# Softmax divided on the product with the values instead of on its own tiles

## The chip, the cores and the metric

The kernel runs on one core of a Trainium2 chip. The metric is the device time of one execution in microseconds (us). TensorE (PE in the rows; PEld is its weight load) multiplies, VectorE (DVE), ScalarE (ACT) and GpSimd (POOL) work element by element, and SyncE (SP) issues the transfers.

## The reference

Attention in which a query sees only the keys of its own hash bucket, and then a feed-forward layer with a convolution along the sequence. B, H, S, D = 4, 8, 768, 64; model width 512, hidden width 1024.

```python
mask = q_bucket[:, :, :, None] == k_bucket[:, :, None, :]
scores = np.where(mask, scale * (q @ k.T), -1e9)
attn = np.exp(scores - scores.max(-1))
attn = attn / (attn.sum(-1) + 1e-9)
x = attn @ v                              # (B, S, H * D)
h = np.maximum(x @ w_in, 0)
gate = sigmoid(conv3(h, conv_w))          # along the sequence, per channel
out = (h * gate) @ w_out
```

## The kernel before

The work is written in one order by hand, and every engine takes its own instructions in that order. A **pair** is two heads of a batch (16 pairs). A **unit** is 128 queries of one head against all 768 keys (192 units, 12 to a pair). The main loop takes one unit a turn and works on three units at once:

- `products` (L250) makes the scores of unit i on TensorE, four matmuls into one of three PSUM buffers "S". The mask is in the product, by extra rows of the operands.
- `maximum` (L258) takes the row maximum on VectorE and writes the scores to SBUF as tile `e`; L262 scales the maximum. `total` (L265) adds 1e-9 to the sum of the unit before.
- `exponential` (L268) is ScalarE's: exp of `e`, with the row sum as a second result.
- `normalise` of unit i-1: the reciprocal of its sum on VectorE (L273), then on GpSimd `e` times it, 128 x 768 (L274).
- `transposes` of unit i-3 (L279) are six transposes of 128 x 128 on TensorE into the next "S" buffer, and `to_sbuf` (L286) is ScalarE's copy of them. Since products and transposes take the three buffers in turn, the transposes of a turn take the buffer which the maximum of the turn before has read.
- Four units (two heads, 256 queries) make one **product with the values**: 24 matmuls of 256 columns (`values`, L299), run in one turn of four (`AVS`). In the next turn ScalarE rounds the result to `xh` (L304), and in the turn after VectorE makes the rest `xl` (L307), at the end of its turn. There are 48 products.

Called by their place against the products, the turns repeat in fours: the first turn after a product with the values, the second (with L307 in it), the third, and the fourth, at whose end the next product runs. In what follows one such four is a **period**.

Beside this run a pair's preparation (`split`, `hash`: GpSimd's L168, L173 and L188, VectorE's L186, transfers) and, until the first feed-forward, the decoding of the 16 weight blocks from float64: VectorE's L88, L90, L92, L94 and L96 on tiles of 128 x 512, ScalarE's L86 and L104, GpSimd's L106 and L108. They are dealt out a step a turn, a block every 4.1 turns, each behind the turn's attention work on the same queues.

The feed-forward of a batch is put off by two pairs (`DEFER`). It runs as one block of work, four times, and takes along (`fill`) the last product with the values of the pair that has just ended. Its hidden part is L324 to L343, its output L354 to L362. The last one follows the last pair, and uses what that pair has just made.

Of the kernel before, what the change touches and what calls it, by code (L numbers as in the profile page):

```python
# [7 lines left out]
F32 = mybir.dt.float32  # L8
# [4 lines left out]
ALU = mybir.AluOpType  # L13

B, H, S, D = 4, 8, 768, 64
NB = 6
DM, DFF = 512, 1024
P = 128
NP = H // 2
NCK = S // P  # L20
HS = S // 2
QB = 256
# [7 lines left out]
LAG, EB = 3, 5  # L30
DEFER = 2
FLAG = 3
AVS = (6, 0, 0, 0)
PREP = (3, 2, 1)
PREP_N = 6
W0 = 6
# [6 lines left out]
def lsh_attention_conv_ffn(ctx, tc, qk, v, hw, w_in, conv_w, w_out, consts, ident_in, out):  # L43
    nc = tc.nc
    PSUM = bass.MemoryType.PSUM
    cp = ctx.enter_context(tc.tile_pool(name="const", bufs=1))
    wp = ctx.enter_context(tc.tile_pool(name="work", bufs=1))
# [4 lines left out]
    def ring(pool, bufs, shape, dtype, tag, name):  # L52

        k = turns[tag] = (turns.get(tag, -1) + 1) % bufs
        return pool.tile(shape, dtype, tag=f"{tag}{k}", name=name, bufs=1)


    ident = cp.tile([P, P], F32, name="ident")
# [51 lines left out]
    def decode_taps(raw):  # L110
        up, low = yield from decode(raw, NFC * 3, "cw")
        nc.vector.tensor_tensor(cw.rearrange("p f k -> p (f k)"), up, low, ALU.add)
# [7 lines left out]
    def fetch(n):  # L120

        for src, name in blocks[:n]:
            raw = cp.tile([P, 2 * WC], I32, tag=f"w{name}", name=f"raw{name}")
            nc.sync.dma_start(raw, src)
            fetched.append((raw, name))
        del blocks[:n]

    def background(rate, stop):

        step[0] += 1  # L130
        if rate and fetched and step[0] // rate > (step[0] - 1) // rate:
            splits.append(split_weight(*fetched.pop(0)))
        now = splits[:]
        while now:
            for g in now[:]:
                ended = next(g, None)
                if ended is None:
                    splits.remove(g)
                if ended is None or ended >= stop:
                    now.remove(g)  # L140
# [97 lines left out]
    class Unit:  # L238
# [11 lines left out]
                    nc.tensor.matmul(self.sp[:, half, :HS], A[:, h, qs], C[:, h, half * HS:(half + 1) * HS],  # L250
                                     start=(kk == 0), stop=(kk == 1))

        def maximum(self, prev):

            self.st = ring(wp, 8, [P, 4], F32, "st", f"st{self.nm}")
            e = wp.tile([P, 776], F32, tag="e", name=f"e{self.nm}", bufs=EB)
            self.e = e[:, :S]
            nc.vector.tensor_scalar(self.e.rearrange("p (a b) -> p a b", a=2), self.sp[:, :, :HS],  # L258
                                    MASKED, None, ALU.max, ALU.max, accum_out=self.st[:, 0:1])
            if prev:  # L260
                prev.total()
            nc.vector.tensor_scalar(self.st[:, 1:2], self.st[:, 0:1], -SCALE, None, ALU.mult)  # L262

        def total(self):
            nc.vector.tensor_scalar(self.st[:, 2:3], self.st[:, 2:3], 1e-9, None, ALU.add)  # L265

        def exponential(self):
            nc.scalar.activation(self.e, self.e, AF.Exp, bias=self.st[:, 1:2], scale=SCALE,  # L268
                                 accum_out=self.st[:, 2:3])

        def normalise(self):
            st = self.st
            nc.vector.reciprocal(st[:, 3:4], st[:, 2:3])  # L273
            nc.gpsimd.tensor_scalar(self.e, self.e, st[:, 3:4], 0.0, ALU.mult, ALU.add)  # L274

        def transposes(self):
            self.tp = ring(ps, 3, [P, 2, 512], F32, "S", f"t{self.nm}")
# [8 lines left out]
            nc.scalar.copy(pr.at[self.h][:, :, :, self.tq * P:(self.tq + 1) * P],  # L286
                           self.tp[:, :, :3 * P].rearrange("p j (c q) -> p j c q", c=3))

    def values(pr, qb, ats):

        if qb == 0:
            pr.x = [ring(wp, NP + DEFER, [P, S], F32R, f"x{k}", f"x{k}{pr.nm}")
                    for k in "hl"]
        vt, (xh, xl) = pr.v, pr.x
        av = ring(ps, 2, [P, 512], F32, "M", f"v{pr.nm}_{qb}")

        def chunk(c):
            for h in range(2):
                nc.tensor.matmul(av[h * D:(h + 1) * D, :QB], vt[:, c, h, :],  # L299
                                 ats[h][:, c // 3, c % 3, :],  # L300
                                 start=(c == 0), stop=(c == NCK - 1), tile_position=(0, h * D))

        def out_high():
            nc.scalar.copy(xh[:, cols], av[:, :QB])  # L304

        def out_low():
            nc.vector.tensor_tensor(xl[:, cols], av[:, :QB], xh[:, cols].bitcast(F32), ALU.subtract)  # L307

        cols = slice(qb * QB, (qb + 1) * QB)
        return [lambda c=c: chunk(c) for c in range(NCK)], (out_high, out_low)  # L310


    g2, prep = [None], [iter(())]
# [54 lines left out]
    def ffn(b, xs, fill, last):  # L368

        gs, acc, run = [], {}, []  # L370
        load_table(AF.Sigmoid)
        todo = [(half, f) for half in range(2) for f in range(NFC)]
        for i in range(len(todo) + FLAG):
            if i < len(todo):
                run.append(hidden(b, *todo[i], xs))
                next(run[i])
            if 1 <= i <= len(todo):
                next(run[i - 1], None)
            if i == 0:
                fill()  # L380
            fetch(1)
            background(HRATE, 2)
            if i >= 3:
                next(prep[0], None)
            if i == len(todo):
                load_table(AF.Exp)
            if i == len(todo) + FLAG - 1:
                last()
            if i >= FLAG:
                output(b, *todo[i - FLAG], gs[i - FLAG], acc)  # L390
            if i < len(todo):
                gs.append(next(run[i]))
            background(HRATE, 2)
# [3 lines left out]
    units = [Unit(pr, t, h) for pr in pairs for qb in range(S // QB) for h in range(2)  # L397
             for t in range(qb * QB // P, (qb + 1) * QB // P)]
# [8 lines left out]
    av, outs, lows, early = [], [], [], None  # L407
    n = len(units)
    ffn_after = {min((b + 1) * NP - 1 + DEFER, B * NP - 1): b for b in range(B)}
    for i in range(n + LAG):  # L410
        u = units[i] if i < n else None
        before = units[i - 1] if 1 <= i <= n else None
        w = units[i - LAG] if i >= LAG else None
        pi, k = divmod(i, 2 * NCK)
        done, outs, lows = lows, [], outs
        for high, low in lows:
            high()
        wi = (i - LAG) // (2 * NCK)
        ending = w and wi in ffn_after and w.qb == S // QB - 1
        if u:  # L420
            u.products()
        if ending:
            for high, low in done + lows:
                low()
            done, lows = [], []
        if u:
            u.maximum(before)
        elif before:
            before.total()
        if w and w is not early:  # L430
            w.transposes()
            w.to_sbuf()
        if u:
            u.exponential()
        if i in (0, 2):
            next(first, None)
        if before:
            before.normalise()
        for high, low in done:
            low()  # L440
        for _ in range(NCK if ending else AVS[(i - LAG) % 4]):
            if av:
                steps, last = av[0]
                steps.pop(0)()
                if not steps:
                    outs.append(last)
                    av.pop(0)
        if u and k == PREP[min(pi, 2)] and pi + 1 < len(pairs):
            prep[0] = pairs[pi + 1].prepare()
        next(prep[0], None)  # L450
        if u and k == PREP[min(pi, 2)] + PREP_N and pi + 1 < len(pairs):
            pairs[pi + 1].load_v()
            if pi + 2 < len(pairs):
                pairs[pi + 2].load()
        if i == 3:
            splits.append(decode_taps(cwr))
        if i >= W0 - 4:
            fetch(i % 4 == 2)
        if i >= 1:
            background(RATE if i >= W0 else 0, 1)  # L460
        if w and w.tq == QB // P - 1 and w.h == 1:
            if not ending:
                av.append(values(w.pair, w.qb, w.pair.at))
            else:
                def fill():
                    steps, last = values(w.pair, w.qb, w.pair.at)
                    for step in [*steps, *last]:
                        step()

                bi = ffn_after[wi]  # L470
                early = units[i + 1 - LAG] if i + 1 - LAG < n else None

                def transposes_ahead():
                    if early:
                        early.transposes()
                        early.to_sbuf()
                        turns["S"] -= 1

                ffn(bi, [pairs[bi * NP + c].x for c in range(NCC)], fill, transposes_ahead)
# [43 lines left out]
```

## Time and profile before

| | |
|---|---|
| median of 3 runs | 774.25 us (772.6 to 776.9) |
| time of the profiled execution | 775.63 us |
| its span, first to last instruction | 773.8 us |
| PE, DVE, ACT, POOL busy | 93%, 65%, 66%, 52% |
| mean granted TensorE clock | 0.98 |

Busy time is a mean over stages with different limits: until 230 us the weights are decoded beside the attention, then four feed-forwards alternate with stretches of attention alone. A wait is read in the stretch where it falls.

### The profile page before, as it was taken

Reading aid. Unit: us, or ns where it says so; the run is one execution under the profiler, and the core shown is the slowest. Engines: PE = TensorE matmul, PEld = TensorE weight load, DVE = VectorE, ACT = ScalarE, POOL = GpSimd, SP = SyncE. Lnnn points to the kernel's source line nnn. Section 1 sums busy time; section 2 is a strip of 40 time slices with the busy share of each in tenths; the row PEclk is TensorE's granted clock in tenths of the full one; section 3 lists DMA queues with packets and bytes.
Section 4 is the critical chain, followed back from the end, with each engine's and each line's share of the span. In section 5 each row is a group of like instructions: output and inputs, shape, how many; then the busy total and the mean of one; then the engine's idle time right before and its main releaser. Section 6 shows DMA issues by size and latency. Waiting matters only on the chain.

```text
span 773.8 us, 13581 instructions
## 1 busy us (share of the span) xinstructions
PE 721.3 (93%) x4552; PEld 586.1 (76%) x4552; DVE 506.7 (65%) x1320; ACT 510.7 (66%) x954; POOL 399.5 (52%) x373
## 2 busy tenths in 40 slices
PE   6968888787889999999999999999999999999997
PEld 3746667565668988777778998777778998778986
DVE  8858988777686665566665655656665665654653
ACT  5857767675665556777775556877776556875453
POOL 4749869595864423557553523466553523441322
PEclk9989999998999999999999999999999999999999
DMA  4565565473631212155452312064452311000011
GB/s 136 141 179 144 153 178 144 135 177 97 153 86 47 62 41 103 38 155 121 119 146 50 82 41 102 19 174 105 132 149 49 82 42 61 1 2 1 1 42 41
DMA packets 30357, 72.18 MB, mean 93 GB/s; under 512 B 5936, under 2 KB 7504, under 8 KB 30288
## 3 DMA queue, kind: packets, MB, share of 16 engines
q1 hardware_dynamic: 30000, 71.27, 33.9%
q8 instruction: 36, 0.59, 0.3%
q14 instruction: 33, 0.27, 0.1%
q10 hardware_dynamic: 288, 0.05, 0.0%
HBM read 27.40 MB, written 6.29 MB: 44 GB/s over the span
## 4 chain that ended last, share of the span: by engine, by line
PE 81%; DVE 10%; issue 3%; DMA 3%; POOL 1%; ACT 1%; SPq 0%; DVEq 0%; POOLq 0%
PE h L324 17%; PE o L354 17%; PE v L299 17%; PE s L250 14%; PE t L279 14%; DVE e L258 5%; DMA R<-in_qk 2%; PE hash L183 2%; DMA k<-R 1%; POOL e L274 1%; DVE wlo L94 1%; DVE wli L94 0%; DVE st L262 0%; DVE st L265 0%; POOL R L173 0%
## 5 line engine op out<-in xcount | busy, mean ns | idle before, releaser
L274 POOL TENSOR_SCALAR e<-e,st 128x768 f32<-128x768 f32 x192 | 179.4, 934 | 184.3 <-ACT at L286 87.2
L258 DVE TENSOR_SCALAR_CACHE_REDUCE e<-s 128x768 f32<-128x768 f32 x192 | 183.1, 954 | 101.5 <-PE s L250 93.6
L268 ACT ACTIVATE e<-e,st 128x768 f32<-128x768 f32 x192 | 180.7, 941 | 42.0 <-DVE st L273 38.5
L286 ACT COPY at<-t 128x768 f32<-128x768 f32 x192 | 151.8, 791 | 63.1 <-PE t L279 62.9
L279 PE MATMUL t<-ident,e 128*128 128x128 f32 x1152 | 165.4, 281 | 28.2 <-DVE st L265 26.2
L279 PEld LDWEIGHTS t<-ident,e 128*128 128x128 f32 x1152 | 132.3, 144 | 55.5 <-issue 30.2
L343 POOL TENSOR_TENSOR g<-ht,g 128x384 fp32r<-128x384 f32 x64 | 72.2, 1128 | 175.2 <-ACT g L342 142.7
L333 DVE SCALAR_TENSOR_TENSOR ht<-ht,cw 128x384 f32<-128x384 f32 (+1 forms) x128 | 113.6, 888 | 71.7 <-ACT ht L331 68.5
L354 PE MATMUL o<-wo,g 128*128 128x512 f32 x576 | 143.0, 395 | 0.0
L324 PE MATMUL h<-xh,wi 128*128 128x386 f32 x512 | 142.0, 340 | 1.0 <-ACT ht L329 1.0
L299 PE MATMUL v<-at,v 128*64 128x256 f32 x1152 | 141.4, 392 | 0.2 <-ACT at L286 0.2
L250 PE MATMUL s<-K,Q 128*128 128x384 f32 x384 | 117.4, 387 | 7.6 <-DVE e L258 4.6
L354 PEld LDWEIGHTS o<-wo,g 128*128 128x128 f32 x576 | 107.4, 188 | 20.8
L299 PEld LDWEIGHTS v<-at,v 128*64 128x64 f32 x1152 | 83.7, 140 | 45.2 <-issue 10.8
L250 PE MATMUL s<-k,q 96*128 96x384 f32 x384 | 100.8, 344 | 2.2 <-DVE e L258 2.2
L324 PEld LDWEIGHTS h<-xh,wi 128*128 128x128 f32 x512 | 94.2, 188 | 5.0 <-ACT ht L329 1.4
L336 ACT ACTIVATE ht<-ht 128x384 f32<-128x384 f32 x64 | 33.6, 525 | 91.2 <-DVE ht L333 91.2
L250 PEld LDWEIGHTS s<-K,Q 128*128 128x128 f32 x384 | 59.5, 194 | 38.0 <-issue 21.9
L324 PE MATMUL h<-xl,wi 128*128 128x386 f32 x256 | 86.9, 339 | 0.0
L250 PEld LDWEIGHTS s<-k,q 96*128 96x128 f32 x384 | 71.6, 193 | 3.0 <-ACT q L230 2.8
L337 DVE TENSOR_TENSOR ht<-ht 128x384 f32<-128x384 f32 x64 | 42.5, 663 | 33.9 <-ACT ht L336 33.9
L173 POOL TENSOR_TENSOR R<-R,hi 128x768 fp32r<-128x768 f32 x30 | 60.3, 2010 | 0.0
(66 smaller groups left out, 591.7 us busy)
## 6 DMA issues: line engine op xcount, KB each, us to landing
R<-in_qk SPq DMA_DIRECT2D x15, 768.0 KB
K<-hi SPq DMA_DIRECT2D x60, 192.0 KB
v<-in_v SPq DMA_DIRECT2D x16, 384.0 KB
out<-osb SPq DMA_DIRECT2D x24, 256.0 KB
Q<-hi SPq DMA_DIRECT2D x30, 192.0 KB
q<-hi SPq DMA_DIRECT2D x30, 192.0 KB
Q<-R SPq DMA_DIRECT2D x30, 192.0 KB
k<-R SPq DMA_DIRECT2D x30, 192.0 KB
```

The lines of the kernel that those rows point to most:

```text
L173: nc.gpsimd.tensor_tensor(lo, R, hi.bitcast(F32), ALU.subtract)
L250: nc.tensor.matmul(self.sp[:, half, :HS], A[:, h, qs], C[:, h, half * HS:(half + 1) * HS], start=(kk == 0), stop=(kk == 1))
L258: nc.vector.tensor_scalar(self.e.rearrange("p (a b) -> p a b", a=2), self.sp[:, :, :HS], MASKED, None, ALU.max, ALU.max, accum_out=self.st ...
L268: nc.scalar.activation(self.e, self.e, AF.Exp, bias=self.st[:, 1:2], scale=SCALE, accum_out=self.st[:, 2:3])
L274: nc.gpsimd.tensor_scalar(self.e, self.e, st[:, 3:4], 0.0, ALU.mult, ALU.add)
L279: nc.tensor.transpose(self.tp[:, c // 3, c % 3 * P:(c % 3 + 1) * P], self.e[:, c * P:(c + 1) * P], ident)
L286: nc.scalar.copy(pr.at[self.h][:, :, :, self.tq * P:(self.tq + 1) * P], self.tp[:, :, :3 * P].rearrange("p j (c q) -> p j c q", c=3))
L299: nc.tensor.matmul(av[h * D:(h + 1) * D, :QB], vt[:, c, h, :], ats[h][:, c // 3, c % 3, :], start=(c == 0), stop=(c == NCK - 1), tile_posi ...
L324: nc.tensor.matmul(hp[:, :HW], w, x[:, c0:c0 + HW], start=(n == 0), stop=(n == 3 * NCC - 1))
L333: nc.vector.scalar_tensor_tensor(t[:, a:z], ht[:, o + k - 1 + a:o + k - 1 + z], cw[:, f, k:k + 1], t[:, a:z], ALU.mult, ALU.add)
L343: nc.gpsimd.tensor_tensor(g[:, 1, :], t, g[:, 0, :].bitcast(F32), ALU.subtract)
L354: nc.tensor.matmul(op, l, r, start=(f == 0 and n == 0), stop=(f == NFC - 1 and n == 2))
```

## The change

The division moves from the tiles `e` to the product with the values. `exponential` writes its sum into a tile `sums` with one column for each of the four units of a product. `total` and `normalise` go. In the second turn after a product, `reciprocals` adds 1e-9 and takes the reciprocal of the four columns on VectorE, and GpSimd spreads each over 64 columns into `rec` (128 x 256). Ahead of a product's matmuls, `spread` transposes `rec` in two transposes into the free half of the product's PSUM bank. ScalarE copies them out (`factors`, in the place of `out_high`), VectorE multiplies the product by them (`out`, in the place of `out_low`), and GpSimd rounds the result to `xh` and makes the rest `xl`.

```diff
+        def reciprocals(self):
+            nc.vector.tensor_scalar(self.sums, self.sums, 1e-9, None, ALU.add)
+            nc.vector.reciprocal(self.sums, self.sums)
+            pr = self.pair
+            pr.rec = ring(wp, 1, [P, QB // P, 2, D], F32, "rec", f"rec{self.nm}")
+            nc.gpsimd.tensor_scalar(pr.rec, self.sums.unsqueeze(3).to_broadcast([P, QB // P, 2, D]), 1.0, 0.0,
+                                    ALU.mult, ALU.add)
-        def total(self):
-            nc.vector.tensor_scalar(self.st[:, 2:3], self.st[:, 2:3], 1e-9, None, ALU.add)
-        def normalise(self):
-            st = self.st
-            nc.vector.reciprocal(st[:, 3:4], st[:, 2:3])
-            nc.gpsimd.tensor_scalar(self.e, self.e, st[:, 3:4], 0.0, ALU.mult, ALU.add)
...
+        def spread():
+            for t in range(QB // P):
+                nc.tensor.transpose(av[:, QB + t * P:QB + (t + 1) * P],
+                                    rec[:, t].rearrange("p h d -> p (h d)"), ident)
-        def out_high():
-            nc.scalar.copy(xh[:, cols], av[:, :QB])
-        def out_low():
-            nc.vector.tensor_tensor(xl[:, cols], av[:, :QB], xh[:, cols].bitcast(F32), ALU.subtract)
+        def factors():
+            nc.scalar.copy(rs, av[:, QB:2 * QB])
+        def out():
+            x = ring(wp, 2, [P, QB], F32, "x32", f"x{pr.nm}_{qb}")
+            nc.vector.tensor_tensor(x, av[:, :QB], rs, ALU.mult)
+            nc.gpsimd.tensor_scalar(xh[:, cols], x, 1.0, 0.0, ALU.mult, ALU.add)
+            nc.gpsimd.tensor_tensor(xl[:, cols], x, xh[:, cols].bitcast(F32), ALU.subtract)
...
+        two = units[i - 2] if 2 <= i <= n + 1 else None
+        if two and two.tq == QB // P - 1 and two.h == 1:
+            two.reciprocals()
         if w and w is not early:
             w.transposes()
             w.to_sbuf()
```

## Rows read from the trace of the kernel before

**Rows 1.** The page: the chain that ended last, by engine.

```profile
PE 81%; DVE 10%; issue 3%; DMA 3%; POOL 1%; ACT 1%; SPq 0%; DVEq 0%; POOLq 0%
```

**Rows 2.** Windows: stretch, its us, busy us of PE, PEld, DVE, ACT, POOL, clock, DMA.

```profile
51.11:230.35 179.24, 147.57 (x1004) 112.09 (x1003) 143.95 (x389) 120.85 (x221) 135.63 (x113) 0.94 0.52 140
...
307.82:773.80 465.98, 459.80 (x2931) 380.44 (x2930) 277.00 (x755) 312.23 (x590) 205.62 (x203) 1.00 0.27 73
```

**Rows 3.** Windows of three single periods, from product to product.

```profile
326.00:334.63 8.63, 8.63 (x66) 6.77 (x68) 5.36 (x22) 6.61 (x14) 6.50 (x8) 1.00 0.45 108
155.59:167.36 11.77, 8.81 (x65) 6.76 (x65) 9.36 (x27) 8.11 (x16) 10.92 (x10) 1.00 0.52 135
179.79:194.30 14.51, 11.93 (x74) 8.06 (x73) 9.38 (x24) 7.67 (x14) 7.49 (x7) 0.84 0.17 55
```

**Rows 4.** Waits from 51 to 231 us: total us, times, longest.

```profile
PE t L279 <- DVE st L265: 26.0, 17, 2.4
...
PE s L250 <- DVE e L258: 4.2, 4, 1.1
```

**Rows 5.** Timeline of one period: start us, us, engine, line.

```profile
160.93 1.08 POOL L274 TENSOR_SCALAR e<-e,st 128x768 f32<-128x768 f32 x1
...
161.26 1.28 DVE L92 SCALAR_TENSOR_TENSOR wuo<-wuo,wlo 128x512 int32<-128x512 int32 x1
...
163.88 1.15 POOL L274 TENSOR_SCALAR e<-e,st 128x768 f32<-128x768 f32 x1 [0.21 <-DVE st L273]
...
164.37 1.19 DVE L96 SCALAR_TENSOR_TENSOR wlo<-rawo,wlo 128x512 f32<-128x512 uint32 x1
...
166.59 0.84 PE L279 MATMUL t<-ident,e 128*128 128x128 f32 x6 [1.48 <-DVE st L265]
```

**Rows 6.** Timeline: L88 while GpSimd ran nothing.

```profile
48.94 0.68 DVE L88 SCALAR_TENSOR_TENSOR wui<-wli,rawi 128x512 f32<-128x512 f32 x1
```

**Rows 7.** Groups on DVE from 51 to 231 us: busy us, mean ns.

```profile
L92 DVE SCALAR_TENSOR_TENSOR wuo<-wuo,wlo 128x512 int32<-128x512 int32 x8 | 10.2, 1280 | 0.3
...
L96 DVE SCALAR_TENSOR_TENSOR wlo<-rawo,wlo 128x512 f32<-128x512 uint32 x8 | 9.6, 1201 | 0.3
```

**Rows 8.** Timeline of an early period: a decoding step and the wait behind it.

```profile
125.18 1.65 DVE L96 SCALAR_TENSOR_TENSOR wli<-rawi,wli 128x512 f32<-128x512 uint32 x1
...
127.84 0.85 PE L279 MATMUL t<-ident,e 128*128 128x128 f32 x6 [2.36 <-DVE st L265]
```

**Rows 9.** Groups of the whole span: the nearest to what is added and removed.

```profile
L274 POOL TENSOR_SCALAR e<-e,st 128x768 f32<-128x768 f32 x192 | 179.4, 934 | 184.3 <-ACT at L286 87.2 <-DVE st L273 84.7 <-PE hash L183 5.1
...
L343 POOL TENSOR_TENSOR g<-ht,g 128x384 fp32r<-128x384 f32 x64 | 72.2, 1128 | 175.2 <-ACT g L342 142.7 <-issue 31.5 <-PE o L354 1.0
...
L273 DVE RECIPROCAL st<-st 128x1 f32<-128x1 f32 x192 | 30.9, 161 | 0.1
L265 DVE TENSOR_SCALAR st<-st 128x1 f32<-128x1 f32 x192 | 28.9, 150 | 13.0 <-ACT e L268 11.6
...
L307 DVE TENSOR_TENSOR xl<-v,xh 128x256 fp32r<-128x256 f32 x48 | 19.6, 408 | 8.3 <-ACT xh L304 8.3
...
L188 POOL TENSOR_SCALAR bits<-bits,cst 128x384 fp32r<-128x384 f32 x15 | 9.2, 613 | 0.0
```

**Rows 10.** Timeline of a period of attention alone.

```profile
330.88 0.85 PE L279 MATMUL t<-ident,e 128*128 128x128 f32 x6
...
331.49 0.59 PE L250 MATMUL s<-K,Q 128*128 128x384 f32 x2
...
332.36 0.41 DVE L307 TENSOR_TENSOR xl<-v,xh 128x256 fp32r<-128x256 f32 x1
...
332.68 0.95 DVE L258 TENSOR_SCALAR_CACHE_REDUCE e<-s 128x768 f32<-128x768 f32 x1
...
333.79 0.85 PE L279 MATMUL t<-ident,e 128*128 128x128 f32 x6
```

**Rows 11.** Timeline ahead of the last feed-forward.

```profile
698.25 0.87 PE L279 MATMUL t<-ident,e 128*128 128x128 f32 x6 [0.85 <-POOL e L274]
```

More of the change, by code (lines that the diff above doesn't have):

```diff
@@ L32 @@
 FLAG = 3
-AVS = (6, 0, 0, 0)
+AVS = (1 + NCK, 0, 0, 0)
 PREP = (3, 2, 1)
@@ L251, in products, with maximum @@
                                      start=(kk == 0), stop=(kk == 1))
-        def maximum(self, prev):
-            self.st = ring(wp, 8, [P, 4], F32, "st", f"st{self.nm}")
+        def maximum(self):
+            self.st = ring(wp, 8, [P, 2], F32, "st", f"st{self.nm}")
+            if self.tq == 0 and self.h == 0:
+                self.pair.sums = ring(wp, 3, [P, QB // P, 2], F32, "sums", f"sums{self.nm}")
+            self.sums = self.pair.sums
             e = wp.tile([P, 776], F32, tag="e", name=f"e{self.nm}", bufs=EB)
@@ L259, in maximum @@
                                     MASKED, None, ALU.max, ALU.max, accum_out=self.st[:, 0:1])
-            if prev:
-                prev.total()
             nc.vector.tensor_scalar(self.st[:, 1:2], self.st[:, 0:1], -SCALE, None, ALU.mult)
-        def total(self):
-            nc.vector.tensor_scalar(self.st[:, 2:3], self.st[:, 2:3], 1e-9, None, ALU.add)
         def exponential(self):
             nc.scalar.activation(self.e, self.e, AF.Exp, bias=self.st[:, 1:2], scale=SCALE,
-                                 accum_out=self.st[:, 2:3])
-        def normalise(self):
-            st = self.st
-            nc.vector.reciprocal(st[:, 3:4], st[:, 2:3])
-            nc.gpsimd.tensor_scalar(self.e, self.e, st[:, 3:4], 0.0, ALU.mult, ALU.add)
+                                 accum_out=self.sums[:, self.tq, self.h:self.h + 1])
+        def reciprocals(self):
[5 more added lines that the diff above has]
+                                    ALU.mult, ALU.add)
         def transposes(self):
@@ L287, in to_sbuf, with values @@
                            self.tp[:, :, :3 * P].rearrange("p j (c q) -> p j c q", c=3))
-    def values(pr, qb, ats):
+    def values(pr, qb, ats, rec):
         if qb == 0:
@@ L301, in chunk @@
                                  start=(c == 0), stop=(c == NCK - 1), tile_position=(0, h * D))
-        def out_high():
-            nc.scalar.copy(xh[:, cols], av[:, :QB])
-        def out_low():
-            nc.vector.tensor_tensor(xl[:, cols], av[:, :QB], xh[:, cols].bitcast(F32), ALU.subtract)
+        def factors():
[5 more added lines that the diff above has]
+            nc.gpsimd.tensor_tensor(xl[:, cols], x, xh[:, cols].bitcast(F32), ALU.subtract)
+        rs = ring(wp, 2, [P, QB], F32, "rs", f"rs{pr.nm}_{qb}")
         cols = slice(qb * QB, (qb + 1) * QB)
-        return [lambda c=c: chunk(c) for c in range(NCK)], (out_high, out_low)
+        return [spread, *(lambda c=c: chunk(c) for c in range(NCK))], (factors, out)
     g2, prep = [None], [iter(())]
@@ L411, in lsh_attention_conv_ffn @@
         u = units[i] if i < n else None
-        before = units[i - 1] if 1 <= i <= n else None
         w = units[i - LAG] if i >= LAG else None
@@ L426, in lsh_attention_conv_ffn @@
         if u:
-            u.maximum(before)
-        elif before:
-            before.total()
+            u.maximum()
+        two = units[i - 2] if 2 <= i <= n + 1 else None
+        if two and two.tq == QB // P - 1 and two.h == 1:
+            two.reciprocals()
         if w and w is not early:
@@ L436, in lsh_attention_conv_ffn @@
             next(first, None)
-        if before:
-            before.normalise()
         for high, low in done:
             low()
-        for _ in range(NCK if ending else AVS[(i - LAG) % 4]):
+        for _ in range(1 + NCK if ending else AVS[(i - LAG) % 4]):
             if av:
@@ L462, in lsh_attention_conv_ffn @@
             if not ending:
-                av.append(values(w.pair, w.qb, w.pair.at))
+                av.append(values(w.pair, w.qb, w.pair.at, w.pair.rec))
             else:
                 def fill():
-                    steps, last = values(w.pair, w.qb, w.pair.at)
+                    steps, last = values(w.pair, w.qb, w.pair.at, w.pair.rec)
                     for step in [*steps, *last]:
```

## The prediction

> **What bounds the kernel now.** I read the chain that ended last first: TensorE carries 81% of it and VectorE 10% [rows 1]. So the question is where VectorE's tenth lies. The windows answer it. After 307 us TensorE is busy 459.8 of 466 us at full clock; in the stretch from 51 to 230 us it is busy 147.6 of 179.2, at a mean granted clock of 0.94 [rows 2]. A period of attention alone takes 8.63 us with no idle TensorE; one of the stretch with the weights takes 11.77 or 14.51 [rows 3]. The waits name the cause there: 26.0 us of the transposes and 4.2 of the scores, both on VectorE's maximum, which frees their PSUM buffer [rows 4]; the small instruction that the row names is only the last that VectorE had done. POOL, whose biggest group the change takes away (179 us, [rows 9]), is 1% of the chain [rows 1]. So the change is worth nothing by POOL's own time. It can matter in two ways: what POOL's work does to VectorE, and what the new steps cost TensorE.
>
> **TensorE: what is added.** Each of the 48 products with the values gets two fp32 transposes of 128 x 128. Six such transposes start at 330.88, and the next scores at 331.49 [rows 10]: 0.61 us, a tenth each. With 0.107 (weight loads and the switch included) 96 of them cost 10.3 us. They stand between a turn's transposes and its product, and nothing covers them: 31 products come after 230 us, where TensorE is full, and in the 15 of the weight stretch the product is a link of the chain too (transposes, product, scores, maximum). Bounds: 0.10 and 0.12 each, 9.6 and 11.5 us. The transposes of a group last 0.85 us from first to last end for six [rows 10], which is pitch plus latency; nobody waits for the latency here, since the product's matmuls write the other half of the bank.
>
> [...]
>
> **VectorE: what is removed.** In the written-out period POOL's `normalise` starts at 160.93 and lasts 1.08; L92 starts at 161.26, inside it, and lasts 1.28. From the end of the POOL instruction at 162.01 to that of L92 at 162.54 is 0.53. L96 does the same: POOL ends at 165.03, L96 at 165.56, again 0.53 [rows 5]. L88, the same form on the same 128 x 512, takes 0.68 alone [rows 6]. So these VectorE steps stand still until the POOL instruction is over, and then need about half a microsecond. In the last eight blocks L92 means 1.280 and L96 1.201 [rows 7], so 0.60 and 0.52 of each is standing still. The maximum of the next turn stands behind them on VectorE, and TensorE behind the maximum: 1.48 us at 166.59 [rows 5].
>
> [...]
>
> What of it comes back? In the later seven periods of the stretch both L92 and L96 are ahead of a wait. L92 gains 0.60. L96 often doesn't: it follows L94, which follows `out` directly, and the new rounding to `xh` goes to POOL just behind `out`. From 613 ns for 384 and 934 for 768 columns [rows 9] that is about 0.5 us on POOL, so L96 meets it in place of `normalise`. I take 0.8 per period with L90's and L94's smaller waits, 5.6 us. In the earlier eight, L92 is hidden by the product, and L96 alone makes the wait: six times 0.6 behind `normalise`, and twice a longer one (1.65 us, then 2.36 of idle TensorE, [rows 8]) behind a POOL weight step that runs late because POOL is backed up; 1.4 each. That is 6.4, and 12 in all. Bounds: if other POOL work moves into the gaps, 5 (the seven L92 and little else); if no VectorE step ever waits, 24, still under the 30.2 of rows 4. POOL itself gives up four `normalise` a period (3.7 us) and takes on about 1.9: 0.5 for `rec`, 0.5 for `xh`, and for `xl` some 0.85, scaled down from 1.128 for 384 columns [rows 9]. All of that has several turns of room, since `x` is read a feed-forward later; for the last pair `xl` of its second block must be there for the tenth matmul or so of the first hidden part, about when it comes.
>
> **VectorE: small steps.** One reciprocal (161 ns) and one addition (150 ns, [rows 9]) a turn become one of each a period. But the four-wide ones sit in the second turn, just the turn with `out`, and there the reciprocal now follows the addition that it depends on, where before L262 stood between them. I put that at 0.12 us later for `out` and for the next maximum. In attention alone that maximum starts at 332.68, behind `xl` (332.36), ends at 333.63, and TensorE's transposes start at 333.79, 0.16 later: TensorE waits for that very maximum. So 0.12 us for each of the 27 such products, 3.2 us, all on the path; 0 if the scores set it instead, 5 if the added dependence costs twice. In the weight stretch it is inside the 12 above. `out` itself has the shape and the PSUM input of `xl` (408 ns), `factors` those of the old rounding: no change.
>
> **Clock.** [...] The drops come where TensorE waits, and not always: one period has a mean of 0.84, and the one from 155.59, with the 1.48 us wait inside it, kept 1.00 [rows 3, 5]. So shorter waits should give some back, not surely all. I take 6, bounds 0 and 10.8.
>
> **The end.** The last transposes wait 0.85 us for the last `normalise` [rows 11]; that goes, and some 0.15 at the restarts: 1.0 us.
>
> **Sum.** 775.6 + 10.3 + 3.2 - 12 - 6 - 1 = 770.1 on the profiled execution, which lies 1.4 above the median of the runs. So about 769.
>
> **The forecast and its rivals.**
> 1. *The forecast*: the waits shrink by half and the clock recovers in part, 769. For: 30 us of waits on VectorE against 13.5 of new cost. Against: the 12 and the 6 are halves of larger bounds. Its own range is 763 to 774.
> 2. *The waits shrink, but the clock stays as it is.* Without the 6 us the sum is 776.1, 775 on the median: no change. For: a wait of 1.48 us left one period at 1.00, so the drops hang on more than the wait's length.
> 3. [...] `xh`, `xl` and the weight steps L106 and L108, which now run as soon as they can, stand in front of L92 to L96. Relief 5, clock 0: 775.6 + 13.5 - 5 - 1 = 783.1, so 782, slower. It decides where the relief is under about 13.5 - 1 = 12.5, clock included. For it: L96 right behind `out`. Against: POOL's load falls by half.
> 4. *VectorE stops waiting at all*, the stretch runs near TensorE's own rate: relief 20, clock 10: 775.6 + 13.5 - 31 = 758, so 757.
> 5. *Each transpose costs its latency*, nearer 0.27 us. Then 96 x 0.27 = 26 in place of 10.3, 785. The six in 0.61 us speak against it; only two alone between other forms for it. [...]
>
> **How the numbers follow.** Chances: case 1 0.52, 2 0.17, 3 0.13, 4 0.13, 5 0.05. Half a per cent, 3.9 us, is about what a measurement of this kernel tells from no change, so the borders are 770.4 and 778.1. Case 1 lies below the first for some 0.40 and inside for 0.12; with 4 faster is 0.53; same is 0.12 + 0.17, and slower 0.18. The range of 757 to 780 leaves out case 5, half of 3 and a part of 4, about 0.18.
>
> **What would show it.** A period of attention alone grows from 8.63 to about 8.95, two new transposes 0.2 us ahead of each product, and the transposes of the fourth turn wait a little longer. L92 falls from 1.28 to 0.68 nearly everywhere, L96 only in part, with POOL's `xh` beside those that don't. The periods from 51 to 230 us become shorter by about 1, the clock there goes above 0.95, and the wait at the last transposes is gone. I am wrong if L92 stays at 1.28, if the attention alone grows by more than half a microsecond a period, or if the first stretch goes on losing as much to VectorE under another name.

## The result, and the profile after

| | before | after |
|---|---|---|
| median of the runs, us (lowest to highest) | 774.62 (772.6 to 776.9, 4 runs) | 764.8 (764.34 to 766.02, 4 runs) |
| span of the profiled execution, us | 773.8 | 761.6 |
| mean granted clock | 0.980 | 0.992 |
| GpSimd busy, us | 399.5 | 294.9 |

The ratio is 0.9875, 95% interval 0.9844 to 0.9905: faster, 4 us below the forecast and inside its range. To see where the 12.2 us of the span went, cut it at two products with the values that both kernels have: the third, and the one in the middle of the first feed-forward.

| stretch | before, us | after, us | change | forecast |
|---|---|---|---|---|
| start to the third product | 51.11 | 46.64 | -4.5 | +0.4 (2 products) |
| third product to the one in the feed-forward | 179.24 | 164.45 | -14.8 | -12 - 6 + 3.2 = -14.8 |
| from there to the end | 543.45 | 550.5 | +7.1 | 6.6 + 3.2 - 1 = +8.8 |

Windows of the changed kernel (columns as in rows 2): the weight stretch, the part after the first feed-forward, and one period of attention alone.

```profile
46.64:211.09 164.45, 144.21 (x1033) 112.09 (x1032) 138.35 (x304) 121.94 (x221) 99.45 (x100) 0.99 0.59 155
288.50:761.60 473.10, 466.90 (x2999) 390.39 (x2997) 265.88 (x586) 313.51 (x593) 147.43 (x177) 1.00 0.27 72
...
336.03:344.95 8.92, 8.88 (x67) 7.08 (x67) 5.07 (x17) 6.74 (x14) 4.02 (x6) 1.00 0.43 103
```

Against [rows 2]: the weight stretch is 14.8 us shorter and its clock went from 0.94 to 0.99. GpSimd's busy time there (the fifth) went from 135.63 to 99.45. Against [rows 3], a period of attention alone grew from 8.63 to 8.92.

Waits of TensorE in the changed kernel from 46 to 212 us (total us, times, longest).

```profile
PE t L280 <- DVE e L260: 14.3, 18, 1.4
PE s L250 <- DVE e L260: 2.7, 4, 1.5
```

These answer to [rows 4]: 30.2 us of waiting for the maximum became 17.0, and the longest single wait 1.5 in place of 2.4. The name of the releaser changed with the order of the small steps; it is the maximum in both.

The chain that ended last, by engine:

```profile
PE 69%; DVE 18%; DMA 5%; ACT 3%; issue 2%; POOL 1%; SPq 1%; DVEq 0%; POOLq 0%; ACTq 0%
```

VectorE's share has gone up from 10% [rows 1] although the kernel is faster and waits less for it. Followed in windows, most of the rise lies in the weight stretch (VectorE's pieces of the chain there go from about 49 to 85 us, while the waits fall); in attention alone, where the maximum now ends last by a quarter of a microsecond in every period without a hash, they go from about 2 to 18. The share says who came last, not by how much; the windows say that.

VectorE's groups from 46 to 212 us, the weight steps (busy us, mean ns).

```profile
L88 DVE SCALAR_TENSOR_TENSOR wuo<-wlo,rawo 128x512 f32<-128x512 f32 x8 | 11.6, 1444 | 9.3 <-ACT wlo L86 9.3
L92 DVE SCALAR_TENSOR_TENSOR wui<-wui,wli 128x512 int32<-128x512 int32 x7 | 10.3, 1478 | 0.2
...
L92 DVE SCALAR_TENSOR_TENSOR wuo<-wuo,wlo 128x512 int32<-128x512 int32 x8 | 8.0, 1006 | 0.3
L96 DVE SCALAR_TENSOR_TENSOR wlo<-rawo,wlo 128x512 f32<-128x512 uint32 x8 | 6.9, 862 | 0.3
...
L96 DVE SCALAR_TENSOR_TENSOR wli<-rawi,wli 128x512 f32<-128x512 uint32 x7 | 4.9, 694 | 0.2
```

In the kernel before, the early L96 was:

```profile
L96 DVE SCALAR_TENSOR_TENSOR wli<-rawi,wli 128x512 f32<-128x512 uint32 x7 | 9.7, 1386 | 0.2
```

L96, and not L92, is the step that came free in the early blocks: 694 ns there (`wli`), all but the 0.68 of L88 alone [rows 6], and 862 in the late ones (`wlo`, 1201 in [rows 7]). L92 is free (0.69) in six of the eight late blocks and in three of the seven early ones; in the other four early ones it takes 1.64 to 2.21, behind a GpSimd step (L108 or L173), and L88 stands behind one everywhere (1.13 to 2.29 us, 0.68 alone in [rows 6]): the splitting of the weights and of the next pair's inputs has moved forward into the time that `normalise` left. It costs little, since L88 and the early L92 run beside TensorE's product, which lasts 2.8 us or more (2.81 in the period below).

The late blocks show the rest of what the forecast feared, in one period of the changed kernel (start us, us).

```profile
151.83 0.57 POOL L316 TENSOR_SCALAR xh<-x 128x256 fp32r<-128x256 f32 x1
...
152.17 0.76 DVE L96 SCALAR_TENSOR_TENSOR wlo<-rawo,wlo 128x512 f32<-128x512 uint32 x1
152.86 0.94 DVE L260 TENSOR_SCALAR_CACHE_REDUCE e<-s 128x768 f32<-128x768 f32 x1
...
153.87 0.88 PE L280 MATMUL t<-ident,e 128*128 128x128 f32 x6 [1.43 <-DVE e L260]
154.58 0.38 PE L301 MATMUL v<-ident,rec 128*128 128x128 f32 x2
154.89 2.81 PE L306 MATMUL v<-at,v 128*64 128x256 f32 x24
```

`xh` sits beside L96 as forecast, but costs it only 0.08 (0.76, against the 0.68 of L88 alone in [rows 6]). The 1.43 us wait that is left is VectorE's own queue: `x`, L94 and L96 ahead of the maximum.

What the new GpSimd steps take (groups of the whole span):

```profile
L317 POOL TENSOR_TENSOR xl<-x,xh 128x256 fp32r<-128x256 f32 x48 | 36.8, 766 | 4.0
...
L316 POOL TENSOR_SCALAR xh<-x 128x256 fp32r<-128x256 f32 x48 | 20.6, 429 | 39.1 <-DVE x L315 34.7 <-DVE sums L270 4.4
L274 POOL TENSOR_SCALAR rec<-sums 128x256 f32<-128x256 f32 x48 | 19.5, 406 | 246.7 <-ACT at L287 146.7 <-DVE sums L271 80.6 <-PE t L280 13.5
```

1.60 us a product, against the 1.85 scaled from [rows 9].

### The profile page after: what moved, and what is told of

It reads as the page before. It is cut to its first block, busy times and chain, and to the rows that moved or that the text cites. A ratio compares the mean times of both kernels' runs of the same rounds, so it can differ in the third digit from the quotient of the medians.

```text
span 761.6 us, 12950 instructions
## 1 busy us (share of the span) xinstructions
PE 722.1 (95%) x4648; PEld 595.3 (78%) x4648; DVE 486.1 (64%) x1032; ACT 511.9 (67%) x954; POOL 294.9 (39%) x325
## 4 chain that ended last, share of the span: by engine, by line
PE 69%; DVE 18%; DMA 5%; ACT 3%; issue 2%; POOL 1%; SPq 1%; DVEq 0%; POOLq 0%; ACTq 0%
PE o L365 18%; PE h L335 17%; PE v L306 14%; PE t L280 10%; DVE e L260 9%; PE s L250 9%; DMA R<-in_qk 2%; ACT at L287 2%; DMA k<-R 2%; DVE x L315 1%; PE hash L183 1%; PE v L301 1%; DVE wuo L92 1%; DVE wlo L96 1%; DVE st L262 1%
## 5 line engine op out<-in xcount | busy, mean ns | idle before, releaser
L280 PE MATMUL t<-ident,e 128*128 128x128 f32 x1152 | 161.5, 277 | 17.4 <-DVE e L260 15.2
L306 PE MATMUL v<-at,v 128*64 128x256 f32 x1152 | 137.0, 383 | 0.0
L274 POOL TENSOR_SCALAR rec<-sums 128x256 f32<-128x256 f32 x48 | 19.5, 406 | 246.7 <-ACT at L287 146.7
L306 PEld LDWEIGHTS v<-at,v 128*64 128x64 f32 x1152 | 82.0, 137 | 41.2 <-issue 7.9
L173 POOL TENSOR_TENSOR R<-R,hi 128x768 fp32r<-128x768 f32 x30 | 58.9, 1964 | 0.7
```

The costliest lines, as they stand in the source:

```text
L173: nc.gpsimd.tensor_tensor(lo, R, hi.bitcast(F32), ALU.subtract)
L280: nc.tensor.transpose(self.tp[:, c // 3, c % 3 * P:(c % 3 + 1) * P], self.e[:, c * P:(c + 1) * P], ident)
```

## The experiments

The theory: the gain is VectorE's weight steps that no longer stand behind GpSimd's pass over `e`, and the cost is the spread plus a later maximum. The rival for the gain: GpSimd was only too busy, and what it reads doesn't matter. The rival for the cost: the spread costs more or less than its pitch.

**Nothing divided at all.** The kernel before without the sum's 1e-9, the reciprocal and the multiplication; its output is the product without the division.

```
         nc.vector.tensor_scalar(self.e..., accum_out=self.st[:, 0:1])
-            if prev:
-                prev.total()
...
-        if before:
-            before.normalise()
```

> The kernel before, without its division (total, reciprocal and normalise left out, so the attention is not divided by its sum). Theory: this is the gain alone, without the new costs. Start 4.5, weight stretch 14.8 and the 4.7 which the spread costs in it, about 3 more since no xh and xl run on GpSimd, 0.9 at the last transposes, 1 elsewhere: 774.6 - 29 = 746 (742 to 753), and a period of attention alone hardly changes (8.5 to 8.65). Rival (transposes wait for the normalise): attention alone falls below 8.4 us a period, and the sum goes under 740.

Measured: 749.16 us, ratio 0.9686 (0.9659 to 0.9714). Windows of its weight stretch and of a period of attention alone:

```profile
49.09:209.89 160.80, 143.55 (x1004) 109.21 (x1003) 131.49 (x271) 121.85 (x222) 73.55 (x54) 0.98 0.60 160
...
330.90:339.34 8.44, 8.44 (x66) 6.89 (x65) 4.73 (x14) 6.50 (x14) 3.11 (x3) 1.00 0.34 85
```

Taking the division away is worth 18.4 us in the weight stretch, beside the 12 + 6 that the forecast gave to relief and clock together. The changed kernel's 164.45 is this 160.80 plus 15 spreads of 0.21 us (3.2) and 0.4: the change gets there nearly all that leaving the division out gives. TensorE still waits 15.5 us for the maximum with nothing divided, and the late L92 still takes 1190 ns, behind GpSimd's L108 and L173 where it is long: these steps hold VectorE as `normalise` did. And TensorE's own period in attention alone is 8.44 (8.41 to 8.50 over the run), so some 0.2 of the 8.63 before [rows 3] was already waiting, although the profile counts TensorE as busy for all of it.

**GpSimd kept busy as before, reading.** The changed kernel, and where `normalise` stood a multiplication of 672 columns of `e` into a scrap tile. `rs` and `x32` have one buffer each to make room.

```
+            nc.gpsimd.tensor_scalar(d, self.e[:, :672], nxt.st[:, 1:2], 0.0, ALU.mult, ALU.add)
```

> The changed kernel, with a GpSimd instruction put back where the old normalise stood: it multiplies 672 of the 768 columns of e by the fresh maximum of the next unit into a scrap tile that nobody reads (output unchanged; rs and x have one buffer instead of two, for room). Theory (VectorE's weight steps stood behind the normalise): the weight stretch goes back from 164 to some 176 us, the start from 46.6 to some 50, L92 from mostly 0.69 back to about 1.2, and the time to 778 (774 to 784). Rival (the gain is that the transposes no longer depend on the normalise, and that VectorE has fewer small instructions): nothing of that comes back, 765 to 767, and L92 stays short or doesn't matter.

Measured: 792.9 us, ratio 1.0258 (1.0218 to 1.0298), slower than was expected, and slower than the kernel before. GpSimd has more to do in it than in the kernel before (154.6 us in the weight stretch against 135.6), since the new steps come on top of the scrap.

**GpSimd kept busy, writing.** The same, but the scrap reads a single column and then writes 672.

```
+            nc.gpsimd.tensor_scalar(d[:, :1], nxt.st[:, 1:2], 1.0, 0.0, ALU.mult, ALU.add)
+            nc.gpsimd.memset(d, 0.0)
```

> As the run that kept GpSimd busy, but the scrap instruction of 672 columns reads nothing: one column waits for the same maximum, then a memset fills the tile. [...] Rival (GpSimd's own work, L106, L108, xh and xl, comes late behind the scrap, and that is what costs): 785 to 795 as with the reading one, L92 and L96 at 1.2 and more. [...]

Measured: 775.41 us, ratio 1.0001 (0.9983 to 1.0019), between the changed kernel (764.8) and the reading scrap (792.9). Windows of the weight stretch and of its part from the eleventh product on, and groups in it, first with the reading scrap:

```profile
52.04:242.39 190.35, 155.87 (x1033) 117.15 (x1032) 147.60 (x298) 120.98 (x221) 154.63 (x158) 0.91 0.49 131
149.60:242.39 92.79, 75.08 (x489) 54.93 (x488) 65.42 (x138) 56.15 (x102) 71.06 (x74) 0.90 0.44 117
...
L270 POOL TENSOR_SCALAR d<-e,st 128x672 f32<-128x672 f32 x59 | 53.4, 905 | 20.8 <-ACT at L291 10.1 <-DVE st L262 9.8 <-ACT e L265 0.6
...
L92 DVE SCALAR_TENSOR_TENSOR wuo<-wuo,wlo 128x512 int32<-128x512 int32 x8 | 9.6, 1196 | 0.3
...
L96 DVE SCALAR_TENSOR_TENSOR wli<-rawi,wli 128x512 f32<-128x512 uint32 x7 | 10.3, 1464 | 0.2
```

and with the writing one:

```profile
52.17:224.30 172.13, 145.23 (x1033) 112.31 (x1032) 134.88 (x300) 121.31 (x222) 147.23 (x217) 0.97 0.54 144
145.00:224.30 79.30, 66.47 (x489) 51.07 (x488) 60.24 (x141) 57.33 (x105) 67.66 (x104) 1.00 0.50 136
...
L271 POOL MEMSET d<- 128x672 f32 x60 | 39.9, 664 | 3.6
L270 POOL TENSOR_SCALAR d<-st 128x1 f32<-128x1 f32 x60 | 15.8, 264 | 11.6 <-DVE st L262 11.2
...
L92 DVE SCALAR_TENSOR_TENSOR wuo<-wuo,wlo 128x512 int32<-128x512 int32 x8 | 5.5, 692 | 0.3
...
L96 DVE SCALAR_TENSOR_TENSOR wli<-rawi,wli 128x512 f32<-128x512 uint32 x7 | 8.8, 1256 | 0.2
```

and of that part in the changed kernel:

```profile
132.28:211.09 78.81, 66.30 (x489) 51.07 (x488) 62.69 (x140) 57.06 (x104) 46.03 (x47) 1.00 0.53 141
```

GpSimd is occupied about as long in both (154.6 and 147.2 us, 905 and 928 ns a turn). The late L92 is at 1196 beside the reading scrap and at 692 beside the writing one. Of the 25.9 us that the reading scrap adds to the weight stretch of the changed kernel (164.45), 18.2 go when it only writes; 7.7 stay. So both have a part, and reading has the larger. The two parts of the stretch tell more. From the eleventh product on the reading scrap adds 14.0 us to the changed kernel's 78.8, with the lower clock that comes with its waits (0.90 against 1.00), and the writing one 0.5; the single buffers of `rs` and `x32`, which both runs have, cost nothing there. The other 7.2 of the 7.7 lie in the early blocks. There four of the seven L96 take 0.69 beside the memset, but three take 1.63 to 2.20 behind GpSimd's L108 or L173, which come late behind the scrap; in the changed kernel all seven take 0.69. So being occupied costs, as far as these rows show, because it pushes other reading steps of GpSimd onto a step that the maximum waits for. Outside the stretch the two are alike: 5.4 and 5.5 us more in the start (some 2.2 of it the clock, as told below), and the rest as long as in the changed kernel to a microsecond.

**No spread.** `out` multiplies by `rec` as it lies, unspread (so by the wrong rows' factors), without the two transposes and `factors`.

```
-            nc.vector.tensor_tensor(x, av[:, :QB], rs, ALU.mult)
+            nc.vector.tensor_tensor(x, av[:, :QB], rec.rearrange("p t h d -> p (t h d)"), ALU.mult)
...
-        return [spread, *(lambda c=c: chunk(c) for c in range(NCK))], (factors, out)
+        return [lambda: None, *(lambda c=c: chunk(c) for c in range(NCK))], (lambda: None, out)
```

> The changed kernel without the two transposes of rec and ScalarE's copy of them; VectorE multiplies the product by rec as it lies (wrong factors, same shape). Theory: the spread costs TensorE 0.25 us a product, so a period of attention alone goes from 8.92 to about 8.67, and the time to 753 (750 to 756). As forecast from the pitch (0.21): 755. Rival (each transpose costs its latency of 0.27 us): 739 and a period of 8.4.

Measured: 758.3 us, ratio 0.9814 (0.9782 to 0.9845): less came back than expected. In its profiled execution, the longest of its four, only the part from the product in the feed-forward to the end is shorter than the changed kernel's (by 4.3 us); the start is 2.3 longer and the weight stretch, at 164.9, no shorter. Its period of attention alone is 8.69, 0.23 under the changed kernel's and 0.25 over the 8.44 without the division. The late maximum is still there and costs nearly as much without the spread.

**The small steps elsewhere.** Four places: the reciprocals in the first turn ahead of the maximum; `out`, `xh`, `xl` in the third turn; the reciprocals in the first turn behind the maximum; and the last two together.

```
+        one = units[i - 1] if 1 <= i <= n else None        # reciprocals, first turn
+        if one and one.tq == QB // P - 1 and one.h == 1:
+            one.reciprocals()
...
-        two = units[i - 2] if 2 <= i <= n + 1 else None
...
-        done, outs, lows = lows, [], outs
+        done, late, outs, lows = late, lows, [], outs      # out, xh, xl: third turn
```

> The changed kernel with reciprocals in the first turn after a product, ahead of the maximum, where VectorE waits for TensorE anyway. Theory (the added dependence pushes out and the next maximum back by 0.1 us, and the transposes of the fourth turn wait for that maximum): a period of attention alone goes from 8.92 to 8.8, the time to 762 (760 to 763.5). Rival (these transposes wait for something else): 8.92 and 764 to 766.

> The changed kernel with out (and so xh and xl) one turn later, in the third turn after a product, behind its maximum. Theory (out stands ahead of the maximum for which TensorE's transposes wait, and xh ahead of L96): a period of attention alone goes from 8.92 to 8.65, some 7 us in all, and the weight stretch is shorter by 2 to 4: 754 (752 to 758). Rival (the period's 0.28 is TensorE's own work): 8.92 stays, 762 to 766.

> The changed kernel with reciprocals in the first turn after a product as in the run before, but behind that turn's maximum, not ahead of it. Theory (ahead of it VectorE waited for the sums, which cost the weight stretch what the attention gained): period of attention alone 8.65, weight stretch as in the changed kernel (164 to 165), 757 to 759. Rival (the place of the reciprocals isn't what lengthened the rest): 762 to 764 again.

> Both: reciprocals in the first turn behind the maximum, out in the third. Theory: TensorE's own 8.43 and 0.21 are all that is left of a period, 8.64, so the second move adds nothing there; in the weight stretch VectorE has one small pair less ahead of L94: 753 to 757. If both gains added up, the period would fall to 8.4, and the time under 750.

| | us | ratio (95%) | period of attention alone | from the product in the feed-forward to the end |
|---|---|---|---|---|
| changed kernel | 764.8 | 0.9875 (0.9844 to 0.9905) | 8.92 | 550.5 |
| reciprocals ahead of the maximum | 763.79 | 0.9874 (0.9852 to 0.9896) | 8.65 | 548.0 |
| `out` in the third turn | 761.91 | 0.9822 (0.98 to 0.9844) | 8.65 | 545.7 |
| reciprocals behind the maximum | 759.57 | 0.9793 (0.977 to 0.9816) | 8.65 | 544.1 |
| both | 760.75 | 0.9805 (0.9784 to 0.9826) | 8.65 | 543.9 |

The rows were not all measured on one chip; each ratio is to the kernel before, measured beside it. Any one of the moves takes the whole wait out of attention alone: 8.65 is 8.44 plus 0.21 for the spread. Ahead of the maximum the gain is lost again elsewhere, and the ratio is the changed kernel's: from product to product the first three feed-forwards take 78.9, 77.2 and 77.2 us, in the changed kernel 78.7, 76.2 and 76.2. The likeliest reason, not tested, is that VectorE then waits for the sums with the maximum queued behind it. The third turn for `out` was expected to shorten the weight stretch too, to 754; the stretch stayed at 165.4. Both moves together bring nothing over the better one.

**Both places, each where it is better.** The reciprocals in the second turn for the first three products and behind the maximum from the fourth; beside it the run behind the maximum again.

```
+        back = 2 if i < 15 else 1
+        one = units[i - back] if back <= i <= n - 1 + back else None
```

> The changed kernel with the reciprocals in the second turn for the first three products (as the change has them) and from the fourth product on in the first turn behind the maximum (as in the run that moved them there throughout). Nothing is left out. Theory: the third product's time of 46.6 us belongs to the order of GpSimd's steps in the start (the bits of the hash ahead of the spreading of the reciprocals), and the 8.65 us period to the place of the reciprocals afterwards, so both are had: start 46.6, weight stretch 162 to 164, rest as with the reciprocals behind the maximum, about 755 to 756 us. Rival: the early third product is a chance of a transfer in the start, not of the order; then the third product comes at 49 to 51 again and the time is 758 to 760.

> The run with the reciprocals in the first turn behind the maximum throughout, once more, beside the one above on the same chip. Nothing is left out. Theory: 759 to 760 us again, third product at 51 us. Rival: if the third product's time is a chance of a transfer, it lies somewhere else this time, by up to 4 us.

Measured: 757.76 us, ratio 0.9787 (0.9761 to 0.9814), and 759.37, 0.9801 (0.9771 to 0.9831). The third product came at 48.99 and 50.64, so the start is 1.7 us shorter in the one order, and the other 2.3 us to the 46.64 of the changed kernel didn't come. The two medians lie as the starts do, but their intervals overlap. Both beat the kernel before and the changed one. Windows of the new one:

```profile
48.99:211.23 162.24, 142.72 (x1034) 110.04 (x1033) 131.67 (x301) 121.70 (x222) 99.19 (x98) 1.00 0.60 156
...
334.52:343.17 8.65, 8.65 (x68) 7.24 (x67) 4.90 (x16) 6.48 (x14) 3.81 (x5) 1.00 0.45 106
```

From 211.23 to its end are 544.4 us. The kernel with nothing divided needs 537.7 there, and 31 spreads of 0.21 make 544.2: with the small steps out of the way the spread is all that the division costs.

How the move does it, first in a period of the changed kernel:

```profile
342.30 0.16 DVE L270 TENSOR_SCALAR sums<-sums 128x4 f32<-128x4 f32 x1
342.50 0.18 DVE L271 RECIPROCAL sums<-sums 128x4 f32<-128x4 f32 x1
342.59 0.41 DVE L315 TENSOR_TENSOR x<-v,rs 128x256 f32<-128x256 f32 x1
...
342.92 0.94 DVE L260 TENSOR_SCALAR_CACHE_REDUCE e<-s 128x768 f32<-128x768 f32 x1
...
343.93 0.87 PE L280 MATMUL t<-ident,e 128*128 128x128 f32 x6
```

and in the same period of the last kernel:

```profile
339.34 0.16 DVE L270 TENSOR_SCALAR sums<-sums 128x4 f32<-128x4 f32 x1
...
339.54 0.18 DVE L271 RECIPROCAL sums<-sums 128x4 f32<-128x4 f32 x1
339.63 0.95 DVE L260 TENSOR_SCALAR_CACHE_REDUCE e<-s 128x768 f32<-128x768 f32 x1
...
340.70 0.42 DVE L315 TENSOR_TENSOR x<-v,rs 128x256 f32<-128x256 f32 x1
...
341.05 0.95 DVE L260 TENSOR_SCALAR_CACHE_REDUCE e<-s 128x768 f32<-128x768 f32 x1
...
342.20 0.82 PE L280 MATMUL t<-ident,e 128*128 128x128 f32 x6
```

In the first, 0.62 us of steps (the addition, the reciprocal and `x`) stand ahead of the maximum on whose end the transposes wait: they start 0.07 us after it. In the second the same reciprocals have gone a turn earlier, behind a maximum that VectorE had time for, and only `x` is left: the transposes start 0.20 us after the maximum's end and no longer wait for it.

## Why the prediction was right

**Relief of VectorE and clock: the sum was right, and a part of the mechanism was the other way round.** Waits for the maximum fell by 13.2 us (forecast 12): by 8.0 up to the eleventh product and by 5.3 behind it, forecast 6.4 for the earlier and 5.6 for the later blocks. Removal of the whole division is worth 18.4 with the clock (forecast 18). But the prediction had L92 come free "nearly everywhere" and L96 "only in part". The early L96 came free and four of the seven early L92 did not: GpSimd's L108 and L173, no longer backed up, moved forward onto L92 and L88, where a product hides them. A step that came free gained what the prediction took or more (the late L92 from 1.28 to 0.69, the early L96 from 1.39 to 0.69; the late L96 only 0.34 of 0.52 on the mean); which step gets it is set by where GpSimd's other work goes. That a reading pass on GpSimd is what costs is shown by the two scraps for 18 us of 26; the other 7.7 comes with GpSimd being occupied, by the rows above because its other reading steps then stand before L96, which the prediction had not priced apart.

**Spread: right.** 0.21 us a product (8.44 to 8.65, in five kernels), forecast 2 x 0.107. The record of a single transpose of the spread lasts 0.273 (median of the 96 of L301), more than twice what one costs. That rules out case 5. The two transposes last 0.38 from first to last end, and nobody waits for that.

**The late maximum: right place, wrong size and count.** The wait was 0.2 a period already and became 0.28: 0.08 more in place of 0.12, and that in the 18 periods of attention alone without a hash, 1.4 us and not 3.2 for 27. With a hash a period mostly went from 9.50 to 9.58, less than the spread costs. What the prediction missed is that most of the old 0.2 had the same cause: before, the transposes of the fourth turn start 0.93 us after the scores ahead of them, in the changed kernel 1.02, and where nothing is divided 0.80. So 6 us, more than it had priced, were to be had by moving two small instructions. The end as a whole grew by 7.1. The terms give 7.0 (6.5 for 31 spreads, 1.4 here, 0.9 back at the last transposes), but from product to product it lies otherwise: 5.3 in the 18 periods, 1.0 in the six with a hash, 1.8 across the three feed-forwards between them, 1.0 back in the periods that end at a feed-forward. That the sum agrees so well is in part luck, and these remainders, of up to 1 us, are unexplained.

**Clock: right.** No run shows by itself what the granted clock takes. Estimated from the means of the windows, at most 0.06 x 179.24 = 10.8 us were lost in the stretch before [rows 2], which is the upper bound of the forecast's 6, and some 0.01 x 164.45 = 1.6 us are lost now; case 2 is out. TensorE's busy time there fell by 3.4 us [rows 2] although 15 spreads came to it, 3.2, so about 6.6 came through the clock (an estimate from these rows; forecast 6).

**The start: missed.** The sum had +0.4 and the trace says -4.5. Two things make it. First, the order on GpSimd. Timeline of the kernel before (one step of GpSimd, and the first of eight DMA issues behind it):

```profile
21.07 0.91 POOL L274 TENSOR_SCALAR e<-e,st 128x768 f32<-128x768 f32 x1 [0.32 <-DVE wucw L88]
21.95 0.59 POOL L188 TENSOR_SCALAR bits<-bits,cst 128x384 fp32r<-128x384 f32 x1
...
23.35 0.86 SPq L192 DMA_DIRECT2D k<-bits  x1
...
46.82 1.51 PE L183 MATMUL hash<-R,hw_sb 128*32 128x384 f32 x8 [3.00 <-DMA R<-in_qk]
```

of the changed one:

```profile
19.65 0.58 POOL L188 TENSOR_SCALAR bits<-bits,cst 128x384 fp32r<-128x384 f32 x1 [1.32 <-DVE bits L186]
20.90 0.87 SPq L192 DMA_DIRECT2D k<-bits  x1
...
44.09 0.85 PE L183 MATMUL hash<-R,hw_sb 128*32 128x384 f32 x8 [2.40 <-DMA R<-in_qk]
```

and of the last one, which has the reciprocals in the second turn here too:

```profile
44.27 1.51 PE L183 MATMUL hash<-R,hw_sb 128*32 128x384 f32 x8 [2.44 <-DMA R<-in_qk]
```

Windows from 42 us to the third product (the column after the five busy times is the clock), of the changed kernel:

```profile
42.00:46.64 4.64, 2.55 (x20) 1.75 (x20) 2.12 (x5) 2.86 (x7) 3.44 (x5) 1.00 0.70 260
```

and of the last one:

```profile
42.00:48.99 6.99, 4.72 (x20) 3.09 (x21) 3.49 (x9) 3.21 (x8) 5.32 (x6) 0.58 0.74 249
```

Before, the bits of the hash wait on GpSimd behind `normalise`, and with them eight DMA issues on SP's queue and, further back in that queue, the load that TensorE's next hash waits for. Without `normalise` the bits are made 2.3 us earlier and the hash runs 2.7 us earlier. Putting the reciprocals in front of the bits again (the run behind the maximum throughout) sends L188 back to 21.60 and the hash to 46.46, which shows the order to be the cause. Second, the clock: in the changed kernel's profiled execution it stays at 1.00 behind the wait for that load, in the last kernel's, after the same wait and with the same steps, it has a mean of 0.58, and hash to product takes 4.72 us in place of 2.55. These 2.2 us belong to that execution and not to the change: among the twelve profiled executions it is the only one in which the clock stays up there, and in the eleven others hash to product takes 3.85 to 4.73 us. So a part of the 4.5 is luck. Without it the span would have shortened by about 10, as the medians did by 9.8.

So of the 4 us between forecast and median the order in the start makes about half, and the smaller price of the late maximum most of the rest.

## What to carry to other kernels

Dividing behind the product trades a pass on GpSimd for transposes on a full TensorE; it paid here because that pass, though itself hidden, held VectorE steps and a DMA queue that TensorE waited for. Price such a pass by what stands behind it in every queue, the start of the kernel included. When small steps are added to an engine that sometimes ends last, put them behind the step that others wait for, in a turn that has room: here two instructions of 0.16 and 0.18 us, moved by one turn, were worth 6 us of the span.

## What the runs showed of the hardware

Beside a GpSimd instruction that only writes (the memset of the writing scrap, 664 ns), VectorE's L92, with two inputs, took 692 ns (mean of the eight late ones; 1196 beside the reading scrap), and four of the seven early L96, with two inputs too, 0.69 us. L94, with one input, did not stay short: its groups have means of 703 and 853 ns in that run, 418 and 417 where nothing is divided. Timeline of the writing scrap:

```profile
153.24 0.66 POOL L271 MEMSET d<- 128x672 f32 x1
153.28 0.90 DVE L94 TENSOR_SCALAR wlo<-wuo 128x512 int32<-128x512 int32 x1
```

It ends 0.28 us after the memset and takes 0.90; where neither a memset nor another large step of GpSimd stands beside it, it takes 0.42 in the same run. It costs little: that part of the stretch is only 0.5 us longer than in the changed kernel.

A wait of TensorE of 2.40 us was followed by a granted clock of 1.00 in the changed kernel's profiled execution (window from 42.00 to 46.64), one of 2.44 us ahead of the same steps by a mean of 0.58 in the last kernel's (42.00 to 48.99), so the clock behind a wait can't be forecast from the wait alone.
